# Searched instruction order, blocks of four tiles, a weight transposed by DMA and softmax products on GpSimd in a two-layer linear-attention and MLP kernel

## The chip, the cores and the metric

The kernel runs on one core of one Trainium2 chip. The metric is the device time of one execution in microseconds (us); a run gives several executions, and I quote the median with the lowest and the highest. The engines are named as in the profile: PE is TensorE (PEld its weight loads), DVE is VectorE, ACT is ScalarE, POOL is GpSimd, SP is SyncE, which issues most DMAs here.

## The reference

2,048 tokens of width 512 pass through attention, MLP, attention, MLP, each with a layernorm before it and a residual sum after it. The attention is linear: there is no score matrix.

```python
x = x + A(layernorm(x)); x = x + B(layernorm(x)); x = x + A(layernorm(x)); x = x + B(layernorm(x))

def A(x):                       # 32 heads of 16
    q, k, v = split(x @ wqkv)
    pq, pk = q @ w_phi, k @ w_phi              # 16x16 per head
    phi_q = concat(softmax(pq), softmax(-pq))  # 32 features per head
    phi_k = concat(softmax(pk), softmax(-pk))
    kv, z = phi_k^T @ v, sum over tokens of phi_k
    return ((phi_q @ kv) / (phi_q @ z + 1e-6)) @ wo

def B(x):                       # F = 1376
    return (relu(x @ W_gate) * (x @ W_up)) @ W_down
```

## The kernel before

The tokens are 16 tiles of 128. For every tile of layer 0 the kernel normalises it (`xn`), turns it so that the width lies on the partitions (`xnTA`), multiplies it with the key weights, which have `w_phi` folded into them once (`K`), takes both exponentials (`ek`), their sums per head (`sk`), and the normalised features (`phiK`), and adds `phiK^T v` into three PSUM banks (`kvz`). Only when all 16 tiles are in can the first tile be attended (queries, `proj`, the residual sum); the MLP (`G`, `Up`, `down`) follows in blocks of tiles.

```python
# per tile, layernorm of the attention
stats: nc.vector.bn_stats / bn_aggr            # mvA
ln:    nc.scalar.activation(ln, mv, func=AF.Ln, bias=eps)
rstd:  nc.scalar.activation(rs, ln, func=AF.Exp, scale=-0.5)
n = op("DVE", SCALE, due, lambda: nc.vector.tensor_scalar(
    out=xn.t[:], in0=x_of(t), scalar1=mv[:, t, 0:1], scalar2=rs[:, t:t + 1], op0=Alu.subtract,
    op1=Alu.mult), [a], [xn], name="xnA", port=True)
...
# per tile, the key features: three ways to share the product between DVE and POOL
if phi_eng == "POOL":
    a = [op("POOL", POOL_PHI, due, lambda: phi(nc.gpsimd, 0, 2), ...)]   # both signs, 1,024 columns
elif phi_eng == "DVE":
    a = [op("DVE", dve(1024), due, lambda: phi(nc.vector, 0, 2), ...)]
else:                                                                    # "BOTH"
    a = [op("DVE", dve(512), due, lambda: phi(nc.vector, 0, 1), ...),
         op("POOL", (965, 975), due, lambda: phi(nc.gpsimd, 1, 1), ...)]
...
keys.tile(t, k0, k0 + p["V0"], k0 + p["Z0"], xT[t], "BOTH")              # layer 0
...
BLOCKS = ((1, 1, 2, 2, 2, 2, 2, 2, 2), (1, 1, 2, 2, 2, 2, 2, 2, 1, 1))   # MLP, tiles per block
...
# every instruction is an Op with an engine, a cost, a due time, dependences and buffers. plan() is a list
# scheduler that models the engines and emits by due time; refine() corrects the due times in ten rounds.
order = refine(ops, ROUNDS)
with tc.manual_schedule():
    for o in order:
        o.emit()
```

So the order of the instructions on each engine is fixed when the kernel is built, from modelled costs. Each engine takes its instructions in that order: one that waits holds up all that stand behind it on its engine.

The softmax here doesn't subtract the row's maximum and nothing guards it: scores larger than these inputs give would overflow.

Of the kernel before, what the change touches and what calls it, by code (L numbers as in the profile page):

```python
# [8 lines left out]
P = 128  # L9
# [139 lines left out]
def back(ops):  # L149


    left = {o: len(o.then) + len(o.behind) for o in ops}
    ready = dict.fromkeys(ops, 0.0)
    clock = dict.fromkeys(HOP, 0.0)
    open_ = {e: [o for o in ops if o.eng == e and not left[o]] for e in HOP}
    for _ in ops:
        best = None
        for e, cand in open_.items():
            if cand:
                at = [(max(clock[e], ready[o] + o.end - o.start - o.spent), o) for o in cand]  # L160
                first = min(t for t, o in at)
                if best is None or first < best[0]:
                    best = first, max((o for t, o in at if t <= first + 1), key=lambda o: (o.start, o.n))
        t, o = best
        clock[o.eng] = t + o.spent
        o.due = -clock[o.eng]
        open_[o.eng].remove(o)
        for d in o.deps:
            left[d] -= 1
            ready[d] = max(ready[d], HOP[o.eng] - o.due)  # L170
            if not left[d]:
                open_[d.eng].append(d)
        for d in o.follow:
            left[d] -= 1
            ready[d] = max(ready[d], d.start + d.spent - d.end - o.due)
            if not left[d]:
                open_[d.eng].append(d)


def refine(ops, rounds):  # L180
    taker = {b: o for o in ops for b in o.takes}
    last = {}
    for o in ops:
        for b in o.takes:
            if b.pool.fifo:
                if b.pool in last:
                    o.follow.append(last[b.pool])
                last[b.pool] = o
    for n, o in enumerate(ops):
        o.n = n  # L190
        o.follow += {taker[b] for b in o.uses} - set(o.deps) - set(o.follow)
        for d in o.deps:
            d.then.append(o)
        for d in o.follow:
            d.behind.append(o)
    best = None
    for k in range(rounds):
        dues = [o.due for o in ops]
        span = max(o.end for o in plan(ops))
        if best is None or span < best[0]:  # L200
            best = span, dues
        back(ops)
    for o, due in zip(ops, best[1]):
        o.due = due
    return plan(ops)
# [31 lines left out]
XPOSE = (1200, 2430)  # L237
RATE = 265.0
# [15 lines left out]
ROUNDS = 10  # L254
BLOCKS = ((1, 1, 2, 2, 2, 2, 2, 2, 2), (1, 1, 2, 2, 2, 2, 2, 2, 1, 1))
# [3 lines left out]
def kernel(  # L259
# [25 lines left out]
    wk, wv, wq, wo = (new(n, [NB, D]) for n in ("wk", "wv", "wq", "wo"))  # L285
# [15 lines left out]
    p_wT = pool("wT", 1, [NB, D])  # L301
# [7 lines left out]
    p_xB = pool("xnTB", 3, [NB, 2 * P], fifo=True)  # L309
    p_h = pool("hT", 2, [NF * 2 * P], fifo=True)  # L310
# [15 lines left out]
    wqkv = A_wqkv.rearrange("(b p) f -> p b f", p=P)  # L326
    x_in = [None] * T
    x_in[0] = load(0, X[0][:, 0, :], xv[:, 0, :], 131072)
    l_wk = [load(0, wk[:, b:b + 2, :], wqkv[:, b:b + 2, D:2 * D], 262144, "ACT") for b in (0, 2)]
    l_wf = load(1, wf[:], A_w_phi.rearrange("(b j) d f -> (j d) b f", b=NB, j=8), 65536)  # L330
    x_in[1] = load(2, X[0][:, 1, :], xv[:, 1, :], 131072)
    l_wv = load(3, wv[:], wqkv[:, :, 2 * D:3 * D], 524288, "ACT")
    op("ACT", (1300, 1300), 5, lambda: nc.scalar.preload_act_table_set("natural_log_exp_and_others"), name="tbl")
    wov = A_wo.rearrange("(h bb c) f -> c h bb f", bb=NB, c=C)
    gv, uv = (w.rearrange("(b p) f -> p b f", p=P) for w in (B_W_gate, B_W_up))
    dv = B_W_down[0:10 * P, :].rearrange("(f p) d -> p f d", p=P)
    l_wq, l_wo, l_wg, l_wu, l_wd = [], [], [], [], []
    late = [("q", wq[:, b, :], wqkv[:, b, 0:D], 131072) for b in range(NB)]
    late += [("g", wg[:, b, :], gv[:, b, :], 352256) for b in range(NB)]
    late += [("o", wo[i * H:(i + 1) * H, :, :], wov[i], 131072) for i in range(C)]  # L340
    late += [("u", wu[:, b, :], uv[:, b, :], 352256) for b in range(NB)]
    late += [("d", wd[:, f:f + 2, :], dv[:, f:f + 2, :], 262144) for f in range(0, 10, 2)]
    late += [("d", wd[:96, 10, :], B_W_down[10 * P:F, :], 98304)]
    homes = dict(q=l_wq, g=l_wg, o=l_wo, u=l_wu, d=l_wd)

    def load_next(after, due):
        if late:
            kind, dst, src, nbytes = late.pop(0)
            homes[kind].append(load(due, dst, src, nbytes, follow=[after]))
# [29 lines left out]
    def fold(w, dst, loaded, due, step, engs):  # L379
        wT = Buf(p_wT)  # L380
        turned, done = [], []
        for m in range(NB):
            ps = Buf(p_b)
            tr = op("PE", mm(4, 128), due + m, lambda m=m, ps=ps: [nc.tensor.matmul(
                ps.t[:, b * P:(b + 1) * P], lhsT=w[:, m, b * P:(b + 1) * P], rhs=ident[:], start=True, stop=True)
                for b in range(NB)], [loaded[m * len(loaded) // NB], c_id], [ps] + ([wT] if m == 0 else []),
                [] if m == 0 else [wT], name="turn")
            turned.append(evac(engs[m % 2], due + m, lambda m=m: wT.t[:, :, m * P:(m + 1) * P],
                               lambda ps=ps: ps.t[:].rearrange("p (b d) -> p b d", d=P), [tr], (), [ps, wT], "wT"))
        for m in range(NB):  # L390
# [3 lines left out]
                start=True, stop=True) for b in range(NB)], [turned[m], c_blk] + turned[:m], [ps], [wT], name="fold")  # L394
# [7 lines left out]
    def turn(src, dst, how, due, after, takes, uses, name):  # L402
        if how == "SP":
            return op("SP", XPOSE, due, lambda: nc.sync.dma_start_transpose(out=dst(), in_=src.t[:]), [after],
                      takes, [src] + uses, name=name, move=500)
# [13 lines left out]
    def norm_A(l, t, due, after, how):  # L419
# [11 lines left out]
        return turn(xn, lambda: xnTA[c][:, :, i * P:(i + 1) * P], how, due, n, [], [], "xnTA")  # L431


    class Keys:
# [6 lines left out]
        def tile(self, t, due, due_v, due_z, xT, phi_eng, v_eng="ACT"):  # L441
# [12 lines left out]
                for b in range(NB)], [xT, l_wv], [vp], name="V")  # L454
# [119 lines left out]
    def mlp(l, t0, n, due_x, due_g, due_d, after, how):  # L574
# [3 lines left out]
        turned = []  # L578
        for i in range(n):
            t = t0 + i  # L580
            a = stats(l, "B", t, due_x(i), [after[t]])
            xc = Buf(p_xn)
# [6 lines left out]
            out=tmp[:, t0:t0 + n], in0=mv[:, t0:t0 + n, 1], scalar1=EPS, scalar2=None, op0=Alu.add), [a], name="ve")  # L589
# [44 lines left out]
        for i in range(n):  # L634
            t = t0 + i
            yp = Buf(p_b)
            last = None
            for lo, hi in ((0, 4), (4, 8), (8, NF)):
                def down(yp=yp, i=i, lo=lo, hi=hi):
                    for f in range(lo, hi):  # L640
                        m = min(P, F - f * P)
                        nc.tensor.matmul(yp.t[:], lhsT=h.t[:m, f * W + i * P:f * W + (i + 1) * P],  # L642
                                         rhs=wd[:m, f, :], start=(f == 0), stop=(f == NF - 1))
                last = op("PE", mm(hi - lo, 512), due_d(i) + lo, down,
                          [made[f] for f in range(lo, hi)] + l_wd + ([last] if lo else []),
                          [] if lo else [yp], [yp, h] if lo else [h], name="down")
            x = x_of(t)
            done.append(op("DVE", dve(512, 1, 130), due_d(i), lambda x=x, yp=yp, t=t: nc.vector.scalar_tensor_tensor(  # L648
                out=x, in0=yp.t[:], scalar=rs[:, t:t + 1], in1=x, op0=Alu.mult, op1=Alu.add), [last, r], (), [yp],
                name="resB"))  # L650
# [6 lines left out]
    for t in range(T):  # L657
        if t == 2:
            x_in[2] = load(4, X[0][:, 2, :], xv[:, 2, :], 131072)
            x_in[3] = load(5, X[0][:, 3, :], xv[:, 3, :], 131072)  # L660
        if t >= 4 and t % 2 == 0:
            x_in[t] = x_in[t + 1] = load(
                p["K0"] + p["KS"] * (t - 5), X[t // C][:, t % C:t % C + 2, :], xv[:, t:t + 2, :], 262144,
                follow=[xT[t - 4]] if t > 6 else [])
        xT.append(norm_A(0, t, p["K0"] - 4000 + p["KS"] * t, [x_in[t]], ("ACT", "DVE")[t % 2] if t < 4 else "SP"))
        if t >= 3:
            load_next(xT[t], p["K0"] + p["KS"] * t)
            load_next(xT[t], p["K0"] + p["KS"] * t)
        k0 = p["K0"] + p["KS"] * t
        keys.tile(t, k0, k0 + p["V0"], k0 + p["Z0"], xT[t], "BOTH")  # L670
    while late:
        load_next(xT[-1], p["K0"] + p["KS"] * T)
    q_fold = fold(wq, Wq2, l_wq, p["QF"], 100, ("ACT", "DVE"))
    eq_free = [[] for _ in range(C)]
    TL = (p["TL0"], p["TL1"])
    for l in range(2):
# [18 lines left out]
        for t0, n, s0 in begin:  # L695
# [4 lines left out]
            for i, a in enumerate(done):  # L700
                t = t0 + i
# [5 lines left out]
                else:  # L707
                    op("SP", (460, 1700), e0, lambda t=t: nc.sync.dma_start(
                        out=ov[:, t, :], in_=x_of(t)), [a], name="store",
                       move=131072 / RATE)  # L710
        xT = nxt

    order = refine(ops, ROUNDS)
# [33 lines left out]
```

## Time and profile before

402.99 us, the median of 3 runs (402.08 to 403.76).

The busy line of the page, by engine: microseconds, share of the span, instructions.

```profile
PE 387.8 (97%) x3176; PEld 265.9 (66%) x3176; DVE 275.5 (69%) x685; ACT 259.5 (65%) x704; POOL 22.1 (6%) x24
```

97% does not say how much PE could still give: matmuls overlap in its pipe, and the Trainium skill (Perfetto Trace Analysis, section "Identifying the Most-Contended Engine") warns of judging by their busy share for that reason. The trace agrees: a matmul of 512 columns is listed with 379 ns, and in a stream the next one starts 216 ns after it. I read the starts of consecutive matmuls from the trace instead. I count columns / 2.4 nanoseconds as what a matmul needs; what the next start is late by is loss. Small losses in a stream, about 2.65 ns on average, come with every matmul; the Trainium skill (TensorE: Matmul & The Clock Gate, section "Wait — 56ns, not 53.3ns?") names about 2.5 ns of fixed cost, and the trace agrees. The whole span is then an exact sum:

| part of the span, us | before |
|---|---|
| until the first matmul | 1.36 |
| columns / 2.4 | 371.73 |
| small loss in streams, under 20 ns each (3,176 matmuls) | 8.48 |
| gaps over 0.1 us | 15.04 |
| gaps between these two sizes | 0.9 |
| after the last matmul's columns | 3.66 |
| span | 401.18 |

The gaps lie in three places: the first 40 us, and the two ramps where attention starts (60 to 80 us and 240 to 280 us). The windows table gives each engine's busy time in a stretch.

```profile
core 0: us, PE busy (x) PEld busy (x) DVE busy (x) ACT busy (x) POOL busy (x), PEclk, DMA share, GB/s
10.00:20.00 10.00, 8.38 (x52) 4.16 (x53) 10.00 (x23) 8.52 (x28) 1.93 (x2) 1.00 0.23 63
20.00:30.00 10.00, 8.40 (x84) 5.32 (x81) 9.88 (x14) 8.02 (x24) 4.86 (x5) 1.00 0.82 190
30.00:40.00 10.00, 9.28 (x57) 4.55 (x56) 9.93 (x23) 8.66 (x28) 2.23 (x2) 1.00 0.73 162
250.00:260.00 10.00, 9.79 (x74) 5.52 (x72) 6.94 (x23) 9.60 (x33) 0.00 (x0) 1.00 0.01 2
```

PE's waits from 5 to 60 us, costliest first (total, times, longest):

```profile
PE b L446 <- DMA xnTA<-xn: 1.8, 2, 1.0
PE b L407 <- DVE xn L427: 1.2, 1, 1.2
PE b L446 <- ACT xnTA L376: 1.2, 2, 0.7
```

L446 is `K`. It waited for the turned tile, once by way of a DMA transpose and once by way of a copy. Two of DVE's groups in the first 60 us (busy, mean ns, idle before it):

```profile
L466 DVE TENSOR_TENSOR phiK<-ek,sk 128x512 bf16<-128x512 bf16 x16 | 12.6, 789 | 0.2
L427 DVE TENSOR_SCALAR xn<-X,mvA,rsA 128x512 bf16<-128x512 bf16 x16 | 7.0, 445 | 0.3 <-DMA xnTA<-xn 0.3
```

From the chain of waits, `G` and `Up` of one block of two tiles, 88 matmuls of 256 columns; and from DVE's timeline, the two last residual sums before the last store (start, duration, in brackets the idle time before it and its releaser):

```profile
137.49 9.61 PE b L607 x88
...
397.08 1.41 DVE L648 SCALAR_TENSOR_TENSOR X<-b,rsB,X 128x512 bf16<-128x512 f32 x2 [0.63 <-PE b L642]
```

### The profile page before, as it was taken

To read this page: it belongs to the slowest core of one execution; us is meant where nothing else is said; L and a number is where in the kernel's file an instruction comes from. 1 tells how busy PE (TensorE), PEld (TensorE's weight loads), DVE (VectorE), ACT (ScalarE), POOL (GpSimd) and SP (SyncE) were. 2 spreads that over 40 slices of the span, in tenths; PEclk is the share of its full clock that TensorE was granted. 3 is DMA by queue.
4 is the path that set the end of the run, shared out by engine and by line. 5 is a ranking of instruction groups with operands and counts; after the bars stand their busy time and mean duration, and the time that the engine had idled before them with its cause. 6 is when DMAs were issued, how large, how long until landed. Compare 5 with 4: busy or idle time off the path is not lost.

```text
span 401.2 us, 8365 instructions
## 1 busy us (share of the span) xinstructions
PE 387.8 (97%) x3176; PEld 265.9 (66%) x3176; DVE 275.5 (69%) x685; ACT 259.5 (65%) x704; POOL 22.1 (6%) x24
## 2 busy tenths in 40 slices
PE   6889999899999999999999999999999999999996
PEld 3454565667787678556777845576778686785784
DVE  6999896999995835787365457799998523132222
ACT  4888999977665355838464759997846353452542
POOL 0142350000000000000000002000000000000000
PEclk9999999999999999999999999999999999999999
DMA  6287940233331013101010100025333102001000
GB/s 211 63 192 159 262 118 0 42 67 63 71 68 41 0 28 67 26 15 28 2 26 2 28 0 2 1 41 81 68 65 68 28 26 68 13 29 39 15 28 28
DMA packets 54536, 21.83 MB, mean 54 GB/s; under 512 B 45952, under 2 KB 53472, under 8 KB 54496
## 3 DMA queue, kind: packets, MB, share of 16 engines
q1 hardware_dynamic: 53424, 20.25, 22.4%
q10 hardware_dynamic: 1072, 1.05, 0.8%
q8 instruction: 25, 0.41, 0.4%
q14 instruction: 15, 0.12, 0.1%
HBM read 8.44 MB, written 2.10 MB: 26 GB/s over the span
## 4 chain that ended last, share of the span: by engine, by line
PE 76%; DVE 14%; DMA 4%; ACT 3%; issue 2%; DVEq 0%; ACTq 0%
PE b L607 35%; PE b L642 18%; PE b L452 5%; PE b L446 5%; PE b L565 4%; PE b L518 3%; PE q L481 3%; DMA xnTA<-xn 3%; DVE pr L558 2%; ACT Eq L522 1%; DVE bstA L416 1%; PE q L536 1%; DVE X L569 1%; DVE m L553 1%; DVE o L561 1%
## 5 line engine op out<-in xcount | busy, mean ns | idle before, releaser
L619 ACT ACTIVATE gu<-b 128x512 bf16<-128x512 f32 (+1 forms) x102 | 55.5, 555 | 61.0 <-PE b L607 60.1
L607 PE MATMUL b<-xnTB,wg 128*128 128x256 bf16 (+3 forms) x836 | 92.9, 256 | 0.4 <-ACT Eq L522 0.3
L607 PE MATMUL b<-xnTB,wu 128*128 128x256 bf16 (+3 forms) x836 | 92.9, 256 | 0.2 <-ACT Eq L522 0.2
L625 DVE TENSOR_TENSOR hT<-gu 128x512 bf16<-128x512 bf16 (+1 forms) x102 | 38.5, 380 | 69.2 <-ACT gu L622 69.0
L642 PE MATMUL b<-wd,hT 128*128 128x512 bf16 (+1 forms) x352 | 82.8, 379 | 0.0
L607 PEld LDWEIGHTS <-wg 128*128 128x128 bf16 (+1 forms) x836 | 72.5, 100 | 11.4 <-issue 0.6
L607 PEld LDWEIGHTS <-wu 128*128 128x128 bf16 (+1 forms) x836 | 72.4, 100 | 8.1 <-issue 0.3
L622 ACT CAST gu<-b 128x512 bf16<-128x512 f32 (+1 forms) x102 | 54.8, 543 | 24.7 <-PE b L607 23.4
L642 PEld LDWEIGHTS <-hT 128*128 128x128 bf16 (+1 forms) x352 | 33.8, 98 | 34.8
L543 ACT CAST N<-q 128x384 bf16<-128x384 f32 (+1 forms) x96 | 48.1, 583 | 0.0
L522 ACT ACTIVATE Eq<-b 128x512 bf16<-128x512 f32 x64 | 40.4, 690 | 5.7 <-PE b L518 5.7
L457 DVE TENSOR_REDUCE sk<-ek 128x64 f32<-128x1024 bf16 x32 | 38.6, 1211 | 6.8 <-ACT ek L449 6.7
L648 DVE SCALAR_TENSOR_TENSOR X<-b,rsB,X 128x512 bf16<-128x512 f32 x32 | 23.3, 745 | 27.5 <-PE b L642 27.4
L449 ACT ACTIVATE ek<-b 128x512 bf16<-128x512 f32 x64 | 35.7, 603 | 8.9 <-PE b L446 8.6
L446 PE MATMUL b<-Wk,xnTA 128*128 128x512 bf16 x128 | 32.3, 380 | 4.2 <-DMA xnTA<-xn 2.1
L466 POOL TENSOR_TENSOR phiK<-ek,sk 128x512 bf16<-128x512 bf16 x18 | 21.4, 1193 | 226.6 <-ACT sk L462 221.9
L565 PE MATMUL b<-wo,oT 128*128 128x512 bf16 x128 | 32.5, 379 | 1.1 <-DVE X L569 0.4
L466 DVE TENSOR_TENSOR phiK<-ek,sk 128x512 bf16<-128x512 bf16 (+1 forms) x32 | 31.2, 977 | 2.4 <-ACT sk L462 2.3
L452 PE MATMUL b<-wv,xnTA 128*128 128x512 bf16 x128 | 32.2, 379 | 0.0
L518 PE MATMUL b<-xnTA,Wq 128*128 128x512 bf16 x128 | 31.7, 379 | 0.0
L543 ACT COPY DS<-q 128x48 f32<-128x48 f32 (+1 forms) x96 | 23.7, 318 | 7.2 <-PE q L536 6.1
L536 PE MATMUL q<-R,Eq 128*128 128x144 bf16 x256 | 25.1, 226 | 0.5 <-ACT N L543 0.4
(65 smaller groups left out, 376.1 us busy)
## 6 DMA issues: line engine op xcount, KB each, us to landing
out_dram<-X SPq DMA_DIRECT2D x16, 128.0 KB, 1.7
X<-in_A_x_dram SPq DMA_DIRECT2D x6, 256.0 KB, 4.0
wg<-in_B_W_gate_dram SPq DMA_DIRECT2D x4, 344.0 KB, 3.8
wu<-in_B_W_up_dram SPq DMA_DIRECT2D x4, 344.0 KB, 3.8
wd<-in_B_W_down_dram SPq DMA_DIRECT2D x5, 256.0 KB, 3.1
wk<-in_A_wqkv_dram ACTq DMA_DIRECT2D x2, 256.0 KB, 3.6
X<-in_A_x_dram SPq DMA_DIRECT2D x4, 128.0 KB, 4.4
wv<-in_A_wqkv_dram ACTq DMA_DIRECT2D x1, 512.0 KB, 5.4
```

The source lines that it names most:

```text
L446: k = op("PE", mm(4, 512), due, lambda: [nc.tensor.matmul(kp.t[:], lhsT=xnTA[c][:, b, cols], rhs=Wk2[:, b, :], start=(b == 0), stop=(b == ...
L452: v = op("PE", mm(4, 512), due_v, lambda: [nc.tensor.matmul(vp.t[:], lhsT=xnTA[c][:, b, cols], rhs=wv[:, b, :], start=(b == 0), stop=(b == ...
L457: a = op("DVE", SUM16, due, lambda: nc.vector.tensor_reduce(out=sk.t[:], in_=ek.t[:].rearrange("p s (h f) -> p (s h) f", f=DH), axis=AX.X, ...
L466: e.tensor_tensor(out=ph.t[:, s:s + n].rearrange("p s (h f) -> p (s h) f", f=DH), in0=ek.t[:, s:s + n].rearrange("p s (h f) -> p (s h) f", ...
L518: q = op("PE", mm(4, 512), due(c, b), lambda b=b, qp=qp: [nc.tensor.matmul(qp.t[:], lhsT=Wq2[:, m, b * P:(b + 1) * P], rhs=xnTA[c][:, m, : ...
L522: done.append(op("ACT", act(512), due(c, b), lambda b=b, s=s, qp=qp: nc.scalar.activation(out=Eq[c][:, b, s, :], in_=qp.t[:], func=AF.Exp, ...
L543: nc.scalar.copy(out=q[:, k, 0:3] if k < 2 else q[:, :, 3], in_=ps.t[:, 0:n * GE].rearrange("p (n c j) -> p n c j", n=n, j=HB)[:, :, lo:hi])
L565: a = op("PE", mm(4, 512), due + 3, lambda: [nc.tensor.matmul(yp.t[:], lhsT=oT.t[:, b, :], rhs=wo[:, b, :], start=(b == 0), stop=(b == NB ...
L607: nc.tensor.matmul(ps.t[:m, q * W:(q + 1) * W], lhsT=w[:, b, g * P:g * P + m], rhs=xT.t[:, b, 0:W], start=(b == 0), stop=(b == NB - 1))
L619: nc.scalar.activation(out=gu.t[:m, 0, lo * W:hi * W], in_=gp.t[:m, lo * W:hi * W], func=AF.Relu)
L622: nc.scalar.copy(out=gu.t[:m, 1, lo * W:hi * W], in_=up.t[:m, lo * W:hi * W])
L642: nc.tensor.matmul(yp.t[:], lhsT=h.t[:m, f * W + i * P:f * W + (i + 1) * P], rhs=wd[:m, f, :], start=(f == 0), stop=(f == NF - 1))
```

## The change

The intent: fewer matmuls, less on DVE in the first 40 us, an earlier first projection, and an order that also holds when the DMA transposes are late. Its core, with cuts marked:

```diff
-def refine(ops, rounds):            # ten rounds on one replay, cut
+def arrange(ops):                   # due times come from a table
+    assert len(ops) == len(DUE)
+        o.n, o.due = n, DUE[n]
+DUE = (12838, 22903, ...)           # 2,072 numbers, found by a search that is not in the kernel
-XPOSE = (1200, 2430)
-RATE = 265.0
+XPOSE, XPOSE_LOADS = (1200, 3600), (1200, 3600)
+RATE = 250.0
-BLOCKS = ((1, 1, 2, 2, 2, 2, 2, 2, 2), (1, 1, 2, 2, 2, 2, 2, 2, 1, 1))
+PHI = ["POOL"] * 15 + ["BOTH"]
+BLOCKS = ((1, 1, 2, 4, 4, 2, 2), (1, 1, 2, 4, 4, 2, 1, 1))
...
-    p_xB = pool("xnTB", 3, [NB, 2 * P], fifo=True)
-    p_h = pool("hT", 2, [NF * 2 * P], fifo=True)
+    p_xB = pool("xnTB", 2, [NB, 4 * P], fifo=True)
+    p_h = pool("hT", 2, [NF * 4 * P], fifo=True)
+    wk, wT_ = (parts of the two hT tiles)          # shortened
...
-    l_wk = [load(0, wk[:, b:b + 2, :], ..., "ACT") for b in (0, 2)]
-    l_wv = load(3, wv[:], wqkv[:, :, 2 * D:3 * D], 524288, "ACT")
+    l_wv = [load(0, wv[:, b:b + 2, :], ..., 262144, "ACT") for b in (0, 2)]
+    l_wk = [load(1, wk[:, b:b + 2, :], ..., "ACT") for b in (0, 2)]
...
+            if by_dma:      # fold: the transposed wq straight from DRAM, no PE and no copies
+                turned.append(op("SP", XPOSE_LOADS, due + m, lambda m=m: nc.sync.dma_start_transpose(
+                    out=wT.t[:, :, m * P:(m + 1) * P], in_=w[m * P:(m + 1) * P, :]), ...))
-        keys.tile(t, k0, k0 + p["V0"], k0 + p["Z0"], xT[t], "BOTH")
+        keys.tile(t, k0, k0 + p["V0"], k0 + p["Z0"], xT[t], PHI[t])
...
+            halves = ((0, 256), (256, 512)) if l == 1 and t == T - 1 else ((0, 512),)   # last down projection
...
-    order = refine(ops, ROUNDS)
+    order = arrange(ops)
```

In the changed kernel `wk` and its transpose lie in the storage of `hT`, so early lines of its profile that say `hT` mean these.

## The prediction

> **What bounds it now.** The page's busy line gives PE 387.8 of 401.2 us (97%), but matmuls are pipelined, so I read consecutive matmul starts in the trace. At 2.4 columns per ns the 3,176 matmuls need 371.7 us. In a stream each starts about 2.65 ns later than columns/2.4, 8.5 us in all; the Trainium skill (TensorE: Matmul & The Clock Gate, section "Wait — 56ns, not 53.3ns?") states about 2.5 ns fixed per warm matmul, and this trace agrees. The rest: 1.4 us before the first matmul, 15 us of gaps over 0.1 us (2 in the cold warm-up matmuls), 3.5 us of tail (two residual additions of 0.70 us, a store of 1.7 us). From 80 to 240 us and after 270 us PE only streams. So there is gain in the first 40 us (9 us of gaps after 5 us), the two ramps where attention starts (70-80 us: 2.3 us; 250-270 us: 2.3 us) and the tail.
>
> In the table of windows DVE is busy 10.0, 9.9, 9.9 of 10 us in 10-40 us, ACT 8.5, 8.0, 8.7; in 40-80 us ACT has 9.5 to 10. In PE's waits the early gaps are xnTA by DMA transpose (2.1 us), xnTA by copies (2.1), xn (1.2).
>
> **What changes.**
> - MLP blocks of four: rhs of 512 instead of 256 columns for eight tiles per layer; 352 fewer matmuls x 2.65 ns = 0.9 us. In the chain 88 matmuls of 256 columns take 9.61 us; I expect 88 of 512 in 18.95 us instead of 19.2.
> - wq transposed by DMA: 16 matmuls of 128 columns go (0.9 us), with two ACT copies (1.2 us) and two DVE copies (1.4 us) of the crowded phase. Four DMA transposes come, each 1.2 us of SP issue and 2.5 us (about 4 us during weight loads) to land; off the path.
> - phiK of layer 0 on POOL: 15 halves of 0.79 us, 12 us, leave DVE. POOL gets 15 x 2.1-2.4 us (estimate: twice the half's 1.05-1.2 us), about 35 us, which fits in 50. ACT becomes the early limit.
> - Value weights first: the first projection starts at 10.2 us today. V needs only the first xnTA (x lands at 3.1 us; stats, scale, turn, copy about 3 us more), not the fold. I expect 6.5-7.5 us.
> - Searched due times, robust to transpose delay: fewer gaps early and in both ramps.
> - The last down projection in halves: 0.4 us off the tail.
>
> **Sum.** PE floor -1.8 us; early gaps from 9 to 4-5 us, -4.5; ramps -1.8; tail -0.4: -8.5 to -9, all on the chain, since PE is the chain from 40 us on. Predicted 394 us (before 403), 80% range 389.5 to 399.5. Faster by over 2%: 0.60; within 2%: 0.39; slower: 0.01. The 2% line is near 395: a close call.
>
> **What would show each step.** About 2,820 matmuls; first V before 8 us; DVE clearly under 9 of 10 in 10-40 us, ACT near 9 or more; POOL over 30 us busy; gaps after 5 us from 13 us to 6-7; G/Up of a four-block 18.95 us; a shorter last store.
>
> **What would make it wrong.** ACT has little more slack than DVE: if it takes over at once, the early gaps only move (397-399). POOL's long instructions could hold up DVE (the skill's SBUF — State Buffer, section "SBUF: two separate sides", describes a shared port pair locked for a whole instruction; no run has shown it yet); then DVE's operations lengthen. Four-tile blocks need four attended tiles before G starts, which may open gaps in the ramps. The other way, the search may close nearly all gaps: 389.

## More of the kernel before

DVE is full from 10 to 40 us and PE is not; in the ramp ACT is, and from 260 us DVE too (9.95 of 10 us from 260 to 270 us, where most of that ramp's gaps lie).

The timeline of the start (start, duration, in brackets the idle time before it and its releaser): the load of `wv` is one DMA, the ACT table comes straight after, and `Wblk` (the block-diagonal `w_phi`, which the fold needs) at 4.97.

```profile
1.74 0.49 ACTq L323 DMA_DIRECT2D wv<-in_A_wqkv_dram  x1
2.26 1.28 ACT L333 ACT_TABLE_LOAD   x1 [2.26 <-issue]
4.10 0.29 ACT L422 ACTIVATE lnA<-mvA,eps 128x1 f32<-128x1 f32 x1 [0.55 <-DVE mvA L417]
4.97 0.69 DVE L361 TENSOR_TENSOR Wblk<-wf,Mf 128x512 bf16<-128x512 bf16 x1 [0.90 <-DMA wf<-in_A_w_phi_dram]
```

## The result, and the profile after

The changed kernel took 398.36 us (398.29 to 399.44, 6 runs); the kernel before took 402.53 (401.65 to 403.76, 6 runs) beside it. The ratio is 0.9899, 95% interval 0.9878 to 0.992. A ratio here is the mean time of one kernel's fast runs over that of the other's of the same rounds, so it is not quite the ratio of the medians that I quote. The time fell by 4.2 us; I had forecast 9. The same sum as before:

| part of the span, us | before | after | difference |
|---|---|---|---|
| until the first matmul | 1.36 | 1.36 | 0 |
| columns / 2.4 | 371.73 | 370.88 | -0.85 |
| small loss in streams | 8.48 | 7.48 (2,819 matmuls) | -1.00 |
| gaps over 0.1 us | 15.04 | 12.16 | -2.88 |
| gaps between | 0.9 | 1.4 | +0.5 |
| after the last matmul's columns | 3.66 | 3.22 | -0.44 |
| span | 401.18 | 396.5 | -4.68 |

By stretch, all losses together went from 9.17 to 7.51 us between 5 and 40 us, and from 6.39 to 6.02 in the two ramps. The floor and the tail came as predicted. The gaps did not go.

The busy line after:

```profile
PE 385.0 (97%) x2819; PEld 232.2 (59%) x2819; DVE 267.1 (67%) x657; ACT 259.2 (65%) x694; POOL 34.2 (9%) x24
```

The windows after:

```profile
core 0: us, PE busy (x) PEld busy (x) DVE busy (x) ACT busy (x) POOL busy (x), PEclk, DMA share, GB/s
10.00:20.00 10.00, 8.88 (x66) 4.69 (x64) 10.00 (x20) 8.94 (x27) 3.82 (x2) 1.00 0.50 127
20.00:30.00 10.00, 9.54 (x63) 5.10 (x62) 10.00 (x17) 7.92 (x26) 5.33 (x3) 1.00 0.53 134
30.00:40.00 10.00, 8.48 (x51) 4.08 (x49) 9.58 (x18) 8.95 (x28) 5.20 (x4) 1.00 0.80 220
250.00:260.00 10.00, 8.65 (x73) 5.12 (x70) 7.93 (x27) 10.00 (x38) 0.00 (x0) 1.00 0.09 15
```

POOL has taken the products over (34.2 us against 22.1), and yet DVE is nearly as full as before from 10 to 40 us. A table of busy time cannot tell work from waiting inside an instruction. The same groups of DVE in the first 60 us can: the products are gone, and the mean `xn` has grown from 445 to 677 ns at the same shape.

```profile
L566 DVE TENSOR_REDUCE sk<-ek 128x64 f32<-128x1024 bf16 x16 | 19.0, 1206 | 5.6 <-ACT ek L558 5.3 <-ACT rsA L532 0.2
...
L535 DVE TENSOR_SCALAR xn<-X,mvA,rsA 128x512 bf16<-128x512 bf16 x16 | 10.4, 677 | 2.1 <-ACT rsA L532 2.1
```

16 `xn` took 7.12 us in all before and 10.84 now, most of it in two that lasted 2.02 us each, at 24.20 and 28.84 us. The longest before was 1.10 us. This is the timeline around the second:

```profile
28.53 2.33 DVE L535 TENSOR_SCALAR xn<-X,mvA,rsA 128x512 bf16<-128x512 bf16 x2
28.61 2.10 POOL L575 TENSOR_TENSOR phiK<-ek,sk 128x1024 bf16<-128x1024 bf16 x1 [2.54 <-PE b L627]
...
30.78 0.23 DVE L525 BATCH_NORM_AGGREGATE mvA<-bstA 128x2 f32<-128x6 f32 x2
...
31.05 0.48 ACT L530 ACTIVATE lnA<-mvA,eps 128x1 f32<-128x1 f32 x2 [1.61 <-DVE mvA L525]
...
31.52 0.56 ACT L479 CAST vext<-b 128x512 bf16<-128x512 f32 x1
...
32.14 1.02 PE L555 MATMUL b<-Wk,xnTA 128*128 128x512 bf16 x4 [1.24 <-ACT vext L479]
```

It reads as a chain. The first line joins two `xn`: the first began before POOL's product and took 0.39 us, the second began at 28.84 with the product running, and ended only at 30.86, 0.15 us after the product. The aggregate of the next tile stands behind it on DVE and is late; ACT sits 1.61 us at `ln`, which waits for it; behind `ln` on ACT stands the copy of `vext`, which empties a PSUM bank; PE waits for that bank with the next `K`. PE's waits from 5 to 60 us show the end of this chain beside the other large one:

```profile
PE b L500 <- DVE Wblk L464: 1.2, 1, 1.2
PE b L555 <- ACT vext L479: 1.2, 1, 1.2
```

The waits of PE for a DMA transpose, 1.8 us before, are gone. The other wait, `Wblk`, comes from the start. There the load of `wv` is two DMAs, and the second was not issued for long (the first line is both), so the table load behind it on ACT slid from 2.26 to 4.26:

```profile
1.75 2.49 ACTq L421 DMA_DIRECT2D wv<-in_A_wqkv_dram  x2
...
4.26 1.28 ACT L435 ACT_TABLE_LOAD   x1 [4.26 <-DMA hT<-in_A_wqkv_dram]
...
5.56 0.29 ACT L530 ACTIVATE lnA<-mvA,eps 128x1 f32<-128x1 f32 x1
...
6.12 0.41 DVE L535 TENSOR_SCALAR xn<-X,mvA,rsA 128x512 bf16<-128x512 bf16 x1 [2.06 <-ACT rsA L532]
...
7.73 0.66 DVE L464 TENSOR_TENSOR Wblk<-wf,Mf 128x512 bf16<-128x512 bf16 x1
...
8.45 1.07 PE L500 MATMUL b<-Wblk,hT 128*128 128x128 bf16 x16 [1.25 <-DVE Wblk L464]
```

DVE stands idle for 2.06 us before the first `xn`, and `Wblk`, behind it on DVE, is 2.8 us later than before. The fold waits for it, and the first `V`, which stands behind the fold on PE, starts at 9.35 us.

The lines that answer to the last two of before, from the chain of waits (`G` and `Up` of a block of four) and from DVE's timeline of the tail:

```profile
138.42 18.99 PE b L717 x88
...
393.16 0.88 DVE L760 SCALAR_TENSOR_TENSOR X<-b,rsB,X 128x256 bf16<-128x256 f32 x2 [0.78 <-PE b L753]
```

88 matmuls of 512 columns in 18.99 us replace two times 9.61 us.

### The profile page after: what moved, and what is told of

The parts are those of the page before. It is cut to its first block, busy times and chain, and to the rows that moved or that the text cites. A ratio compares the mean times of both kernels' runs of the same rounds, so it can differ in the third digit from the quotient of the medians.

```text
span 396.5 us, 7594 instructions
## 1 busy us (share of the span) xinstructions
PE 385.0 (97%) x2819; PEld 232.2 (59%) x2819; DVE 267.1 (67%) x657; ACT 259.2 (65%) x694; POOL 34.2 (9%) x24
## 4 chain that ended last, share of the span: by engine, by line
PE 74%; DVE 12%; ACT 4%; issue 2%; DVEq 0%
PE b L717 35%; PE b L753 17%; PE b L561 5%; PE b L555 5%; PE b L674 4%; PE b L627 4%; PE q L590 3%; DVE X L678 2%; ACT Eq L631 2%; DVE bstB L524 2%; DVE pr L667 2%; PE q L645 1%; DVE o L670 1%; ACT N L652 1%; DVE m L662 1%
## 5 line engine op out<-in xcount | busy, mean ns | idle before, releaser
L717 PE MATMUL b<-xnTB,wu 128*128 128x128 bf16 (+4 forms) x660 | 89.7, 279 | 0.1
L717 PE MATMUL b<-xnTB,wg 128*128 128x128 bf16 (+5 forms) x660 | 89.3, 279 | 0.0
L729 ACT ACTIVATE gu<-b 128x512 bf16<-128x512 f32 (+4 forms) x98 | 54.6, 572 | 51.4 <-PE b L717 50.8
L735 DVE TENSOR_TENSOR hT<-gu 128x512 bf16<-128x512 bf16 (+4 forms) x98 | 37.9, 392 | 71.2 <-ACT gu L732 70.8
L753 PE MATMUL b<-wd,hT 128*128 128x512 bf16 (+2 forms) x363 | 83.2, 373 | 0.0
L732 ACT CAST gu<-b 128x512 bf16<-128x512 f32 (+3 forms) x98 | 54.3, 563 | 37.6 <-PE b L717 36.9
L717 PEld LDWEIGHTS <-wg 128*128 128x128 bf16 (+1 forms) x660 | 55.0, 100 | 25.4
L575 POOL TENSOR_TENSOR phiK<-ek,sk 128x1024 bf16<-128x1024 bf16 (+1 forms) x18 | 33.5, 1878 | 211.7 <-DVE sk L566 185.1
L760 DVE SCALAR_TENSOR_TENSOR X<-b,rsB,X 128x512 bf16<-128x512 f32 (+1 forms) x33 | 23.0, 726 | 23.2 <-PE b L753 23.2
L645 PEld LDWEIGHTS <-Eq 128*128 128x128 bf16 x256 | 19.2, 98 | 8.2 <-issue 0.9
```

The costliest lines, as they stand in the source:

```text
L645: pe.append(op("PE", mm(len(groups), GE), due, lambda ps=ps, groups=groups: [nc.tensor.matmul(ps.t[:, n * GE:(n + 1) * GE], lhsT=Eq[c][:, ...
L717: nc.tensor.matmul(ps.t[:m, q * W:(q + 1) * W], lhsT=w[:, b, g * P:g * P + m], rhs=xT.t[:, b, 0:W], start=(b == 0), stop=(b == NB - 1))
L729: nc.scalar.activation(out=gu.t[:m, 0, lo * W:hi * W], in_=gp.t[:m, lo * W:hi * W], func=AF.Relu)
L732: nc.scalar.copy(out=gu.t[:m, 1, lo * W:hi * W], in_=up.t[:m, lo * W:hi * W])
L753: nc.tensor.matmul(yp.t[:, 0:c1 - c0], lhsT=h.t[:m, f * W + i * P:f * W + (i + 1) * P], rhs=wd[:m, f, c0:c1], start=(f == 0), stop=(f == N ...
```

## The experiments

The theory, called A: POOL's product and the `xn` of DVE exclude each other for a whole instruction, and whichever asks first goes first. The Trainium skill (SBUF — State Buffer, section "SBUF: two separate sides") describes such a lock on a port pair that DVE, in some of its operations, shares with GpSimd. The rivals: the early part is simply full, so that ACT or DVE only hands its waiting on (the prediction's own doubt); the table load at the start costs it; the gain of the search itself is small or is eaten by the slower engines. D is the theory for the ramps: ACT, full there, is their limit. Where a quoted expectation uses another letter, what it expects is told with it.

The four batches each ran on one chip, with the kernel before beside them; its medians were 403.24, 403.03, 402.16 and 403.34 us, its ratios are per batch. Two levels turned up in the fast runs: executions whose mean granted clock is given as 0.994 to 0.996 are 0.9 to 1.6 us longer than those of the same kernel at 0.999 or 1.00 (the kernel before 1.6 to 2.4 us). Where it matters I compare within a level ("full clock": 0.999 and over). The kernel before had 402.54, 402.95 and 402.22 us as full-clock means in the first three batches.

| run | what differs | median us (range) | ratio to before (95%) |
|---|---|---|---|
| after_again | nothing, the changed kernel | 398.49 (398.38–398.61) | 0.9875 (0.9845–0.9906) |
| guard | products on POOL wait for the `xn` before them | 396.51 (395.7–397.71) | 0.9831 (0.9795–0.9867) |
| tbl | table load before the second `wv` | 397.65 (397.43–397.93) | 0.9855 (0.9824–0.9885) |
| nosearch | old ten rounds instead of the table of due times | 400.1 (399.51–400.74) | 0.9915 (0.9883–0.9948) |
| both | guard and tbl | 395.33 (394.89–395.61) | 0.9803 (0.9781–0.9826) |
| best | both, and `Wblk` earlier | 395.75 (394.84–397.01) | 0.9818 (0.9793–0.9844) |
| walk | `xn` read and written in steps | 406.57 (405.98–407.63) | 1.0085 (1.0062–1.0109) |
| ns_both | nosearch, products shared as before | 403.2 (401.91–405.14) | 1.0003 (0.9974–1.0032) |
| ramp1 | both, `oT` copies of the ramp on DVE | 396.81 (396.58–398.28) | 0.9867 (0.9847–0.9887) |
| ramp2 | ramp1, `xnTB` copies too | 399.18 (398.62–400.98) | 0.9926 (0.9906–0.9947) |
| halves | products on POOL in two instructions | 398.01 (396.86–398.59) | 0.9889 (0.9872–0.9906) |
| ns_oldblocks | nosearch, blocks of two | 403.48 (403.24–404.43) | 1.0033 (1.0014–1.0051) |
| lighteq | both, half of layer 1's query exponentials (wrong) | 394.95 (394.73–395.38) | 0.9799 (0.977–0.9827) |
| both_again | both, on another chip | 395.47 (394.76–395.7) | 0.9806 (0.9777–0.9834) |

### after_again: is the long `xn` an accident?

The changed kernel again, no edit.

> The changed kernel once more, as the yardstick of this batch: ratio to the kernel before 0.990 (0.988 to 0.992), span 396 to 397 us, two xn operations of DVE stretched from 0.40 to about 2.0 us (near 24.2 and 28.8 us). If those two stretches are an accident of one execution and not of the order of instructions, they will lie elsewhere or be gone.

398.49 us, span 396.8, and the two long `xn` came at the same two places, 24.48 and 29.13 us. Not an accident of one execution.

### guard: make POOL ask second

```diff
-                e.tensor_tensor(
+                return e.tensor_tensor(
 ...
+        last = None
         for o in order:
-            o.emit()
+            made = o.emit()
+            if o.name == "xnA":
+                last = made
+            if o.name == "phi" and o.eng == "POOL" and last is not None:
+                tc.add_manual_dep(made.ins, last.ins.name, mybir.DependencyInfo(
+                    mybir.DependencyClass.Sync, mybir.DependencyReason.DATA), reason="lock order")
```

No data need this wait. In the order in which the kernel emits its instructions the `xn` stand before the product; on the chip POOL had got ahead of DVE. The edit makes the chip keep the order; it only adds a wait.

> Only change: each phiK instruction of POOL also waits, by a semaphore, until the xn operation that stands before it in the planned order is done. Theory A (POOL's phiK, 1.93 us long, twice gets ahead of an xn that should go first, holds DVE up by 1.6 us each time, DVE's statistics then hold up ACT and PE): no xn over 1.0 us before 40 us, the 1.4 us gap of PE near 30.5 us gone, big PE gaps between 20 and 40 us from 2.6 us to 1 us or less, span 394 to 395 us (ratio to before about 0.984). Theory B (ACT is full there, or the transposes are late, and the stretched xn only fills time that DVE would have waited): the stretches go, but the span stays at 396 to 397 us.

396.51 us; at full clock 395.91 (3 runs), 2.6 us less than the changed kernel's 398.49, and at the reduced clock 397.29 (3). The `xn` group of DVE in the first 60 us:

```profile
L535 DVE TENSOR_SCALAR xn<-X,mvA,rsA 128x512 bf16<-128x512 bf16 x16 | 6.9, 463 | 2.1 <-ACT rsA L532 2.1
```

The mean is back from 677 to 463 ns, the longest `xn` is 0.91 us. The timeline of the same stretch:

```profile
27.11 0.72 DVE L535 TENSOR_SCALAR xn<-X,mvA,rsA 128x512 bf16<-128x512 bf16 x2
...
28.01 1.93 POOL L575 TENSOR_TENSOR phiK<-ek,sk 128x1024 bf16<-128x1024 bf16 x1 [1.12 <-DVE mvA L525]
...
28.25 0.54 ACT L530 ACTIVATE lnA<-mvA,eps 128x1 f32<-128x1 f32 x2
...
29.45 1.89 PE L555 MATMUL b<-Wk,xnTA 128*128 128x512 bf16 x8
```

Two `xn` take 0.72 us together, the product follows them, ACT does not wait at `ln`, and PE runs eight matmuls of `K` in 1.89 us without a gap. Between 20 and 40 us the gaps over 0.1 us fell from 2.60 us to none, and all losses from 5 to 40 us from 7.51 to 5.09. A wait that was added took 2.6 us off the time: theory A stands, and "simply full" falls for this part. DVE did not become free by it: it was busy 10.0, 10.0 and 9.2 of 10 us from 10 to 40 us with guard too, and only from 40 to 60 us did it have room (10.4 of 20 us busy, 18.3 in the kernel before). What changed is which instruction waited, not how full DVE was.

### tbl: the table load where it was

```diff
+    table = next(o for o in order if o.name == "tbl")
+    order.remove(table)
+    order.insert(max(order.index(a) for a in l_wv), table)    # before the second half of wv is issued
```

> Only change: ACT loads its function table before, not after, it issues the second half of wv, an issue that is held up until 3.9 us in the changed kernel. Theory C (the first layer-norm scale waits for the table, so DVE idles 2.06 us before the first xn and everything after it in DVE's order, the mask product Wblk too, is 1.4 us late): the first ln at about 4.2 instead of 5.56 us, first xn at 4.8 instead of 6.12, PE's gap of 1.5 us before the fold mostly gone, and 0.8 to 1.4 us off the span if the crowded phase passes it on. Rival: DVE, full from 10 to 40 us, or the arrival of x and wk eats it: span within 0.4 us of the changed kernel's.

397.65 us, 0.8 less than the changed kernel. The timeline of the start:

```profile
2.26 1.28 ACT L435 ACT_TABLE_LOAD   x1 [2.26 <-issue]
...
6.89 0.66 DVE L464 TENSOR_TENSOR Wblk<-wf,Mf 128x512 bf16<-128x512 bf16 x1
```

The table is back at 2.26 and `Wblk` comes 0.84 us sooner. A gap of 1.39 us before the fold remains: `Wblk` still stands behind an `xn` and its neighbours on DVE. The start cost 0.8 us through the table, not all of its gap.

### nosearch: without the searched due times

`refine` of the kernel before, ten rounds, in place of the table `DUE`; everything else as changed.

> Only change: the table of searched due times is taken out; the due times come from the ten rounds of the kernel before, on the new instructions. If the search itself (robust to transpose delays) is what gained the 4 us, this is back at 400 to 401 us. If the new instructions gained it (POOL for phiK, blocks of four, wq by DMA), it stays at 396.5 to 398.5 us. With the old planning I expect waits of PE for DMA transposes to come back (2.1 us in the kernel before, none in the changed one).

400.1 us; at full clock 399.59 (3 runs) against 398.49: the searched table gave 1.1 us. I had expected waits for DMA transposes to come back on PE; none did. Long `xn` came here as well, three of them, the longest 2.03 us: the lock is not the search's doing. The profiled execution shows what the reduced clock is (PE's timeline):

```profile
8.65 1.83 PE L406 MATMUL b<-Wblk,hT 128*128 128x128 bf16 x16 [1.46 <-DVE Wblk L370]
10.27 1.91 PE L467 MATMUL b<-wv,xnTA 128*128 128x512 bf16 x4
```

The same fold took 1.07 us in the changed kernel, and four matmuls of `V` 1.03: from 8.7 to 12.2 us, 3.4 us after the gaps of the start, the matmuls ran at half speed again (granted clock 0.52 from 8.62 to 12.03 us). The Trainium skill (TensorE: Matmul & The Clock Gate, section "What's actually happening") tells of a gate that halves the clock after an idle window, with a free-running window of about 3.4 us, so that executions differ. The trace agrees in length, and so do the other kept traces at a reduced clock: halves and ns_both (both 0.996) have one such stretch of 3.4 us at the start, walk (0.991) has two. That the free-running window picks the executions is argued, not shown. Half speed for 3.4 us costs at most 1.7 us (an estimate, from that page's window); that covers the 0.9 to 1.6 us between the levels here, but not the up to 2.4 us of the kernel before, of which no trace at the reduced clock was kept.

### both, both_again: the two repairs together

The edits of guard and tbl.

> The changed kernel with both edits: POOL waits for the xn before it, and the table is loaded early. If the two losses are separate terms of one chain they add: ratio to before about 0.979, span 393.2 to 393.6 us (394.2 with the wait alone, minus 0.9 to 1.2 for the table). If the early start is only absorbed by DVE, which is full from 10 to 40 us, span stays at 394.0 or more.

> The run with both edits once more, as the yardstick for the run beside it and as a second measurement of the fastest version: 394.9 to 395.7 us at full clock, ratio to before 0.979 to 0.982, PE's big gaps between 240 and 270 us about 2.2 us, apart from missing records.

395.33 and 395.47 us on two chips, all at full clock, ratios 0.9803 and 0.9806: 3.2 us less than the changed kernel of the first batch, which ran on another chip (measured at full clock against the kernel before of each batch, 3.6 and 3.1 us), where guard and tbl alone gave 2.6 and 0.8. Within what the chips differ by, they add up. This is the best version found; it beats both kernels.

### best: `Wblk` earlier as well

```diff
+    order.remove(c_blk)
+    order.insert(next(k for k, o in enumerate(order) if o.name == "aggr") + 1, c_blk)   # on top of both
```

> As the run before, and the mask product Wblk comes right after the first layer-norm statistics in DVE's order, in place of behind the second tile's. PE's gap of 1.4 to 1.6 us before the fold should shrink below 0.7 us; 0.3 to 1.0 us off the span of the run before, so 392.3 to 393.2 us, ratio about 0.977. If the first fold then waits for the transposed wk instead, or DVE passes nothing on, no gain.

395.75 us, 395.47 at full clock against 395.27: no gain. The gap before the fold shrank from 1.3 (both) and 1.6 us (both_again) to 0.96 us, but another of 0.89 us opened at 6.35, since the first `xn` now waits behind `Wblk`. The work at the start moved; it did not shrink.

### halves: shorter instructions on POOL

```diff
-                a = [op("POOL", ..., lambda: phi(nc.gpsimd, 0, 2), ...)]
+                a = [op("POOL", ..., lambda: [phi(nc.gpsimd, k, 1) for k in (0, 1)], ...)]
```

> The changed kernel (span 396.5 to 396.8 us), each phiK of POOL in layer 0 as two instructions of 512 columns, in the same order and without added waits. If an xn that comes second has to wait for a whole POOL instruction, it now waits for half as long: the longest xn falls from 2.0 to about 1.1 us, and 1 to 1.7 us come off the span. If POOL's second half goes first again, xn stays at 2.0 us and the span does not change; POOL has 0.1 to 0.2 us more per tile.

The longest `xn` was 1.17 us instead of 2.02 (others 1.15, 1.14, 1.07), and one piece on POOL took 1.08 us. That confirms that an `xn` waits for one POOL instruction, whatever its length. In time it is inconclusive: 398.01 us, but five of six executions were at the reduced clock; the one at full clock took 396.86, 1.6 less than the changed kernel.

### walk: can `xn` be kept off the lock?

```diff
+        def walk(ap):
+            return ap.rearrange("p (a b) -> p b a", b=32) if l == 0 and t >= 5 else ap
-            out=xn.t[:], in0=x_of(t), ...
+            out=walk(xn.t[:]), in0=walk(x_of(t)), ...
```

Reading and writing in steps of 32 elements should take the `xn` of tiles 5 to 15 out of the fast mode, which I supposed to be what needs the shared ports.

> The changed kernel, with xn of tiles 5 to 15 of layer 0 read and written in steps of 32 elements, which should cost DVE its fast mode for them: about 0.6 instead of 0.40 us each, 2.2 us more DVE work in all. If what stretches xn is the port that DVE's fast mode shares with POOL (Trainium skill, SBUF - State Buffer, section SBUF: two separate sides), no xn lasts over 0.75 us although POOL's phiK still runs beside them, and PE's gap near 30.5 us goes; span 394.5 to 396.5 us. If POOL or the semaphores delay DVE in another way, stretches of 2 us stay and the span is 397 to 399 us.

406.57 us, and the expectation was wrong twice. An unblocked `xn` took 1.38 to 1.41 us, not 0.6, and blocked ones up to 3.24. The products on POOL were held up in turn (first 60 us):

```profile
L577 POOL TENSOR_TENSOR phiK<-ek,sk 128x1024 bf16<-128x1024 bf16 x13 | 30.8, 2384 | 28.5 <-ACT sk L573 27.2 <-PE q L592 1.1
```

Their mean was 2,384 ns instead of 1.93 us. So the exclusion goes both ways, and a stepped access does not end it. Whether the `xn` left its fast mode at all is not known from this run, so it does not tell what in `xn` asks for the lock.

### ns_both: is the product on POOL a gain at all?

```diff
-PHI = ["POOL"] * 15 + ["BOTH"]
+PHI = ["BOTH"] * 16          # on top of nosearch
```

> Of the changed kernel without the searched times (400.1 us), only phiK undone: every tile of layer 0 is shared by DVE and POOL again. If moving phiK to POOL gains what it takes off DVE in spite of the blocking, this is 2 to 3.5 us slower, 402 to 403.5 us. If the blocking eats the whole gain, it is within 1 us of 400.1.

403.2 us, all six executions at a reduced clock. The three at 0.995 and 0.996 average 402.32 us, against nosearch's 400.66 (3 executions at 0.994 to 0.996, in the batch before, on a chip where the kernel before was 0.4 us faster at full clock): 1.3 to 1.7 us slower like for like. The other three, at 0.986 to 0.99, were longer still. PE waits for DMA transposes, 1.6 us, are back. Taking the products off DVE was a gain even with the lock in it; it was not free, as I had costed it.

### ns_oldblocks: what do blocks of four cost the ramps?

```diff
-BLOCKS = ((1, 1, 2, 4, 4, 2, 2), (1, 1, 2, 4, 4, 2, 1, 1))
+BLOCKS = ((1, 1, 2, 2, 2, 2, 2, 2, 2), (1, 1, 2, 2, 2, 2, 2, 2, 1, 1))   # on top of nosearch
```

> Of the changed kernel without the searched times (400.1 us), only the blocks undone: MLP blocks of two again. By the count of matmuls alone it should be 352 x 2.6 ns = 0.9 us slower, 401.0 us; if blocks of four also cost or save waits in the ramps, it is off that by 0.5 us or more.

403.48 us, 3.8 slower than nosearch at full clock (403.38 against 399.59). 0.9 us of that is the small loss of the added matmuls (7.48 to 8.42 us). The rest is no price of blocks: the order came out otherwise everywhere, the 16 `xn` took 15.7 us in all, and a gap of 2.31 us opened at 44.5. So this run doesn't give a clean price, and a cost of blocks of four to the ramps stays unmeasured.

### ramp1, ramp2 and lighteq: is ACT the limit of the ramps?

The early `oT` copies (ramp1) and then also the early `xnTB` copies (ramp2) go from ACT to DVE, on top of both:

```diff
-            (nc.scalar.copy if eng == "ACT" else nc.vector.tensor_copy)(out=out_(), in_=in_())
+            act = eng == "ACT" and name not in ('oT',)            # ramp2: ('oT', 'xnTB')
+            (nc.scalar.copy if act else nc.vector.tensor_copy)(out=out_(), in_=in_())
```

> On top of the run with both edits (395.3 us, span 393.8): the copies of oT of the first two tiles of each layer, four in all, go to DVE at their planned places. Theory D (ACT is the limit of both ramps: it is busy 9.8 to 10.0 of 10 us there while DVE has 7 to 8, so the ramps could gain little from a new order): PE's gaps of 0.80 us before the projection at 63.4 us and 0.73 us at 255.8 us shrink to 0.3 us or less, 0.5 to 1.5 us off the span. Rival: the chain of one attended tile (ACT copies, six DVE operations, transpose, projection) is the limit, not ACT's occupancy; then the gaps only move to the next step and the span changes by less than 0.3 us.

> As the run before, and the four early copies of xnTB also go from ACT to DVE. If ACT limits the ramps, another 0.2 to 0.8 us off; if not, nothing or a loss of up to 0.5 us because DVE is full from 70 us on.

Both were slower than the run both: 396.81 and 399.18 us against 395.33 (in another batch). In ramp2 PE waits 2.3 us for the `oT` copies on DVE in the ramps. Relieving ACT moved the wait to DVE (the copies kept the places that had been planned for them on ACT). One execution of ramp1, the profiled one, took 1,042.82 us, with most matmuls of 512 columns 0.62 us from the next at a granted clock of 1.00. It is left out of the figures and unexplained, so ramp1 has no trace of a usual execution.

lighteq takes work from ACT without giving it to anyone. Its output is wrong, which doesn't matter for the time.

```diff
-                    out=Eq[c][:, b, s, :], in_=qp.t[:], func=AF.Exp, ...
+                    out=Eq[c][:, b, s, 0:n], in_=qp.t[:, 0:n], func=AF.Exp, ...   # n = 256 in layer 1, else 512
```

> A wrong result on purpose. On top of the run with both edits (395.3 us, span 393.8): in layer 1 the 32 exponentials of the queries write 256 of 512 columns, about 0.2 us less ACT time each, 6.8 us in all; the order, the waits, PE's and DVE's work stay. Theory D (ACT's occupancy limits the second ramp): PE's big gaps between 240 and 270 us fall from 2.2 us to 0.8 or less and 1.2 to 2 us come off the span. If the chain of one attended tile limits the ramp, the gaps stay within 0.5 us of 2.2 us and the span within 0.5 us.

394.95 us against 395.47 for both_again of the same batch. The windows of both_again, then those of lighteq (columns as above):

```profile
240.00:250.00 10.00, 9.95 (x70) 5.60 (x70) 5.54 (x14) 9.78 (x29) 2.99 (x2) 1.00 0.00 1
250.00:260.00 10.00, 8.58 (x79) 5.37 (x78) 9.62 (x31) 10.00 (x37) 0.00 (x0) 1.00 0.10 15
```

```profile
240.00:250.00 10.00, 9.95 (x70) 5.59 (x70) 4.95 (x15) 7.22 (x28) 3.06 (x2) 1.00 0.00 1
250.00:260.00 10.00, 8.65 (x88) 5.78 (x88) 9.65 (x31) 9.37 (x35) 0.00 (x0) 1.00 0.11 19
```

ACT came into the ramp with 2.6 us of room and left it unused: PE is as idle as before (8.65 against 8.58 of 10), and the losses from 240 to 280 us are 4.35 against 4.62 us. (Both figures hold 1.3 us that is no loss: in each trace the records of six matmuls are missing there, which look like gaps of 0.22 us.) Of the 0.7 us between the spans of the two profiled executions, 0.4 us was there before 240 us, where the edit changes nothing. Theory D falls for the second ramp.

What theory D overlooked is DVE. From its first operation on an attended tile (`m`, at 248.83 us in both_again and 248.37 in lighteq) DVE works through its list with no pause over 0.11 us until past 270 us: busy 9.62 and 9.65 of 10 us in the table, 10.0 from 260 to 270 us in both. The list runs from 250 to 261 us at the same spacing in both runs, 0.5 us earlier in lighteq, so DVE was not waiting for ACT in either. The runs ramp1 and ramp2 gave DVE more work and lost time. All this points to DVE as what sets the pace of the ramp; no run took work off DVE there, so it is not shown.

## Why the prediction was right or wrong

The time lies in the predicted range (389.5 to 399.5), but at its slow end: I gave "faster by over 2%" the best chance, and it was 1%. Point by point:

- **PE's floor, -1.8 us: right.** Columns -0.85 and small losses -1.00 make -1.85. The block of four took 18.99 us, predicted 18.95; 2,819 matmuls, predicted about 2,820.
- **Tail, -0.4 us: right.** It went from 3.66 to 3.22.
- **"Early gaps from 9 to 4-5 us, -4.5": this is the step that failed.** All losses from 5 to 40 us fell by 1.7 us only. The step said that 12 us of products leave DVE and that DVE would be clearly under 9 of 10; DVE stayed at 10.0, 10.0 and 9.6, and gave back 3.7 us to long `xn` (10.84 against 7.12). I counted the work that leaves DVE at its full length and the lock at nothing, though I named the lock among the doubts. What it cost is measured: 2.6 us of time, by guard. With guard all losses from 5 to 40 us are 5.09 us, 4.1 below the kernel before: without the lock the step would have given nearly its 4.5. The mark that I had set for it was wrong for another reason: DVE is at 10.0, 10.0 and 9.2 with guard as well, and its room comes after 40 us. The late table at the start cost 0.8 more, by tbl. It was in the diff (one load became two ahead of the table load) and I did not see it.
- **First `V` before 8 us: wrong.** 9.35 us; "V needs not the fold" is true of its data, but it stood behind the fold in PE's order, and the fold waited for `Wblk`.
- **"Ramps, -1.8 us": wrong.** -0.4 measured. ACT's load does not explain it in the second ramp (lighteq). DVE, without a pause there, is the likely limit (both_again, lighteq), but no run tested it; the cause of the shortfall is open, and so is what blocks of four cost there.
- **Robust due times: right in direction.** PE's waits for DMA transposes went from 1.8 us to none, and the search gave 1.1 us in all. But nosearch had no such waits either, so the search is not shown to be what removed them.
- **"ACT takes over": wrong as the reason.** ACT was at 8.9, 7.9 and 9.0 of 10 in 10 to 40 us, and its largest idle times there were waits for DVE's late aggregates (3.0 us in all). With guard it was at 9.6 and 10.0 from 20 to 40 us, and PE had no gap over 0.1 us there.

With both repairs the kernel takes 395.3 to 395.5 us, 7.7 less than the kernel before in the same batch (403.03 to 395.33). The missing 1.3 us to my 394 are about the size of the ramps' shortfall (1.4 us); that these are the same is an inference.

## What to carry to other kernels

Work moved from DVE to POOL is not gone from DVE if the two exclude each other instruction by instruction: look at the longest instance of each DVE operation beside POOL's instructions, since a busy share of 10 of 10 hides it, and if a short one is stretched, make the long POOL instruction ask second, even at the price of a wait that no data need. When a diff splits one DMA into two, look at what stands behind the second issue on its queue's engine, a table load above all. Cost a change by the chain that ends last in each stage, and ask of every microsecond taken off an engine who will wait next.

## What the Trainium skill lacked or had wrong

- SBUF — State Buffer: the lock that it describes fits what was seen. The page already says, in its section "Who interferes with whom", that the order of issue decides who is held up and which DVE operations can be; the runs agree (beside POOL's products the `xn`, TENSOR_SCALAR in bf16, was stretched; the sums, TENSOR_REDUCE, 1.18 to 1.22 us, never were). It lacks what this can cost a whole kernel, and that an added wait can set the order. Here an `xn` of 0.40 us became 2.02 behind a product of 1.93 us, and a wait that keeps the order gained 2.6 us.
- SBUF — State Buffer: it gives no times for a stepped operation under the lock. A stepped `xn` (steps of 32 elements) was held up still (up to 3.24 us), held up POOL too (2.38 us instead of 1.93), and cost 1.40 us instead of 0.40.
- TensorE: Matmul & The Clock Gate: the page's section "HAM oscillation — how this bites in real kernels" ties the return to half speed to gaps over about 3.4 us. In nosearch the matmuls were at half speed again from 8.7 to 12.2 us (four of `V` in 1.91 us instead of 1.03) after waits of 0.66 and 1.46 us with little work between them. (The page also tells of another kernel in which short idle times bring it about, but gives no length for them.) Executions with a mean granted clock of 0.994 to 0.996 were 0.9 to 2.4 us longer, as much as many of the differences studied here.
- No page gives a length for it: a second issue of `wv` on ACT's DMA queue was held, and ACT with it: two issues of `wv`, where one takes 0.49 us, lasted 2.49 us, about 1.5 us too long; the table load slid by 2.0 us. What held it the runs do not show.
- No page: one execution of 1,042.82 us with most matmuls of 512 columns 0.62 us apart at a granted clock of 1.00.
